# A reordered set-up and an earlier GRN total in a tuned ConvNeXt-V2 block on one Trainium2 core

## The chip, the cores and the metric

The kernel runs on one core of one Trainium2 chip. The metric is device time of one execution in microseconds (us). Each kernel is executed several times, and a median and a range are given. TensorE is called PE in the profile (PEld is its weight load), VectorE DVE, ScalarE ACT, GpSimd POOL, SyncE SP. The three queues that issue transfers here are SPq, ACTq and POOLq.

## The reference, cut to what matters

```python
# x: 1 x 512 x 512 x 96, bfloat16; dw 3x3x96; w1 96x384; w2 384x96
h = depthwise_conv3x3(x, dw)
h = layernorm(h)                     # over the 96 channels, no scale or shift
h = gelu_tanh(h @ w1)                # 96 -> 384
gx = sqrt(sum(h*h over H, W) + 1e-6) # one number per channel, over the whole image
nx = gx / (mean(gx) + 1e-6)
h = gamma * (h * nx) + beta + h      # GRN
return x + h @ w2
```

GRN is the knot: no output can be made before every pixel has passed the GELU.

## The kernel before

The image is cut into 128 blocks of four rows. **Phase 1** (to about 990 us) runs a software pipeline with one block a slot: x is transposed by DVE (`turn_x`), PE convolves with tap weights (`Wq`, three bursts of 24 matmuls), ACT copies the result to `y_bf` and squares it, PE sums both into `SG`, a short chain makes the reciprocal deviation `rstd`, and the norm multiplies `y_bf` by `rbc`, the deviation spread to all channels. The first four blocks (the ramp) spread `rstd` through PE; later ones send it out to DRAM (`r_dram`) and read it back broadcast (`rbc`). The normed block goes through DRAM into `ynT`, and the first expansion (`w1p`) and the GELU follow. **Phase 2** recomputes some expansions, multiplies by `W2s` (w2 with the GRN scale) into `O`, adds the residual `xb` made by POOL, and writes.

The parts that the change touches (cut):

```python
FILL = (6, 24)                       # dummy matmuls that keep PE's clock up
...
act.dma_start(out=dw9[:], ...)
for b in range(2): load_x(b)         # on the SP queue
# w1, w2, gamma, beta by act.dma_start, then the GELU table warm-up
for b in range(2, 4): load_x(b)
make_identity(nc, ident_f[:])
pool.memset(Wq[:], 0.0)
for t in yn_ring:                    # six tiles, zero rows 96..127
    pool.dma_start(out=t[C:128, :, :], in_=zrow[...])
...
n += 1                               # twelve tap copies Wd -> Wq
(dve if n % 2 else pool).tensor_copy(out=Wq[...], in_=Wd[...])
...
def setup_mlp():                     # called after slot 1
    dve.memset(w1p[C:128, :], 0.0)
    Us = psY.tile([128, NI, W], f32, name="Y")   # the convolution's own PSUM tile
    # w1m, b2_ps by PE; w1p and B2bc_f copied out by DVE
...
def stage_norm(b):                   # every block
    pool.tensor_tensor(out=yn[:], in0=ybf.pop(b)[:], in1=rbcs[k][...], op=ALU.mult)
...
for n in range(RES):                 # end of phase 1
    for f in recompute_units(ORDER[n]): f()
advance(LEAD, PRE)                   # lead expansions of phase 2
# then: sums over blocks, rsqrt, total over channels (PE), W2s, B2c, all on DVE
```

Of the kernel before, what the change touches and what calls it, by code (L numbers as in the profile page):

```python
# [8 lines left out]
ALU = mybir.AluOpType  # L9
# [3 lines left out]
GR = 4  # L13
# [3 lines left out]
FILL = (6, 24)  # L17
BATCH = 4
RES = 2
# [34 lines left out]
def kernel(  # L54
# [105 lines left out]
    with ExitStack() as p1:  # L160
# [8 lines left out]
        def banks(n):  # L169
            return (psU2 if n == 2 else psU1).tile([128, n, W], f32, name=f"U{n}")  # L170
# [33 lines left out]
        for b in range(min(2, NBLK)):  # L204
            load_x(b)
        for i in range(NI):
            act.dma_start(out=w1_raw[i:C:NI, :], in_=w1[chans(i), :])
# [4 lines left out]
        act.activation(out=warm[:], in_=warm[:], func=ACTF.Gelu_apprx_tanh)  # L212
        for b in range(2, min(4, NBLK)):
            load_x(b)
        make_identity(nc, ident_f[:])
        pool.memset(Wq[:], 0.0)
        for t in yn_ring:
            pool.dma_start(out=t[C:128, :, :], in_=zrow[C:128, None, :].to_broadcast([128 - C, GR, W]))
# [5 lines left out]
        dve.memset(cen[:], 1.0)  # L224
# [127 lines left out]

        busy(FILL[0])
# [9 lines left out]
        for h in range(2):  # L363
            for j in range(GR):
                for q in (2 * h, 2 * h + 1):
                    a = q + GR * shift(h, j) - j + 1
                    if 0 <= a < 3:
                        n += 1
                        (dve if n % 2 else pool).tensor_copy(out=Wq[32 * q:32 * q + 32, :, :, j, :],
                                        in_=Wd[32 * q:32 * q + 32, :, 3 * a:3 * a + 3, :])  # L370

        def setup_stats():
            dve.memset(SG[:], 0.0)
            dve.memset(rowsel[:], 0.0)
            for j in range(GR):
                dve.memset(rowsel[32 * j:32 * j + 32, j:j + 1], 1.0)

        def setup_mlp():
            dve.memset(w1p[C:128, :], 0.0)
            Us = psY.tile([128, NI, W], f32, name="Y")  # L380
            w1m, b2_ps = Us[:, 0, :E], Us[:, 1, :C]
            pe.matmul(w1m, lhsT=cen[:], rhs=w1_raw[:], start=True, stop=True)
            for j in range(NCH):
                pe.matmul(b2_ps, lhsT=bet_bf[:, j:j + 1].to_broadcast([128, 128]), rhs=w2_sb[:, j, :],
                          start=(j == 0), stop=(j == NCH - 1))
            dve.scalar_tensor_tensor(out=w1p[:C, :], in0=w1m[:C], scalar=-1.0 / C, in1=w1_raw[:],
                                     op0=ALU.mult, op1=ALU.add)
            dve.tensor_copy(out=B2bc_f[:], in_=b2_ps)
# [200 lines left out]
        def stage_norm(b):  # L589
            k = batch_of[b]  # L590
            b0, n = BATCHES[k]
            yn = ynpool.tile([128, NI, W], bf16, name="yn")
            pool.tensor_tensor(out=yn[:], in0=ybf.pop(b)[:],
                               in1=rbcs[k][:, b - b0:b - b0 + 1, :].to_broadcast([128, NI, W]), op=ALU.mult)
            yns[b] = yn
# [132 lines left out]
        setup_stats()  # L728
        store = None
        for s in range(last_slot + 1):  # L730
# [26 lines left out]
            def spread_out():  # L757
                for k in get("spread"):
                    stage_spread(k)
                for b in get("norma"):  # L760
                    stage_norm(b)
# [67 lines left out]
            if s == 1:  # L829
                setup_mlp()  # L830
# [17 lines left out]
        if store:  # L848
            store()
        for j in range(NCH):  # L850
            junk = bstpool.tile([128, 128], f32, name="junk")
            dve.scalar_tensor_tensor(out=junk[:], in0=gram[:, j, :], scalar=1.0, in1=ident_f[:],
                                     op0=ALU.mult, op1=ALU.mult, accum_out=diag[:, j:j + 1])

        for n in range(RES):
            for f in recompute_units(ORDER[n]):
                f()
        made[0] = RES * UPB
    with p2:
        late.psU2 = p2.enter_context(tc.tile_pool(name="psU2", bufs=2, space=bass.MemoryType.PSUM))  # L860
        dve2, pe2, psO = dve, pe, late.psO
        advance(LEAD, PRE)
        gsm = p2.enter_context(tc.tile_pool(name="gsm", bufs=1))
        m2 = gsm.tile([128, NCH, NACC], f32, name="m2")
        dve2.tensor_tensor(out=m2[:], in0=mv[:, :, :, 0], in1=mv[:, :, :, 0], op=ALU.mult)
        dve2.tensor_tensor(out=m2[:], in0=m2[:], in1=mv[:, :, :, 1], op=ALU.add)
        dve2.tensor_tensor(out=m2[:], in0=m2[:], in1=npx[:, None, :].to_broadcast([128, NCH, NACC]), op=ALU.mult)
        ssq = gsm.tile([128, NCH], f32, name="ssq")
        dve2.tensor_reduce(out=ssq[:], in_=m2[:], axis=AX.X, op=ALU.add)
        dve2.scalar_tensor_tensor(out=ssq[:], in0=ssq[:], scalar=GRN_EPS, in1=diag[:], op0=ALU.add, op1=ALU.add)  # L870
        gi = gsm.tile([128, NCH], i32, name="gi")
        dve2.tensor_scalar(out=gi[:], in0=ssq[:].bitcast(i32), scalar1=-0.5, scalar2=float(0x5F3759DF),
                                op0=ALU.mult, op1=ALU.add)
        r = gi[:].bitcast(f32)
        for it in range(3):
            t_ = gsm.tile([128, NCH], f32, name=f"gt{it}")
            dve2.scalar_tensor_tensor(out=t_[:], in0=r, scalar=-0.5, in1=r, op0=ALU.mult, op1=ALU.mult)
            dve2.tensor_tensor(out=t_[:], in0=t_[:], in1=ssq[:], op=ALU.mult)
            rn_ = gsm.tile([128, NCH], f32, name=f"gr{it}")
            dve2.scalar_tensor_tensor(out=rn_[:], in0=t_[:], scalar=1.5, in1=r, op0=ALU.add, op1=ALU.mult)  # L880
            r = rn_[:]
        gx = gsm.tile([128, NCH], f32, name="gx")
        rs_ = gsm.tile([128, 1], f32, name="rs_")
        dve2.scalar_tensor_tensor(out=gx[:], in0=ssq[:], scalar=1.0, in1=r, op0=ALU.mult, op1=ALU.mult,
                                       accum_out=rs_[:])
        tot_ps = psO.tile([128, GPS, C], f32, name="O")[:, 0, 0:1]
        pe2.matmul(tot_ps, lhsT=ones_f[:], rhs=rs_[:], start=True, stop=True)
        den = gsm.tile([128, 1], f32, name="den")
        dve2.tensor_scalar(out=den[:], in0=tot_ps, scalar1=1.0 / E, scalar2=GRN_EPS,
                                op0=ALU.mult, op1=ALU.add)  # L890
        gg = gsm.tile([128, NCH], f32, name="gg")
        dve2.tensor_tensor(out=gg[:], in0=gx[:], in1=gam[:], op=ALU.mult)
        rden = gsm.tile([128, 1], f32, name="rden")
        dve2.reciprocal(out=rden[:], in_=den[:])
        sc = gsm.tile([128, NCH], f32, name="sc")
        dve2.tensor_scalar(out=sc[:], in0=gg[:], scalar1=rden[:, 0:1], scalar2=1.0, op0=ALU.mult, op1=ALU.add)
        for j in range(NCH):
            dve2.tensor_scalar(out=W2s[:, j, :], in0=w2_sb[:, j, :], scalar1=sc[:, j:j + 1], scalar2=None,
                                    op0=ALU.mult)
        dve2.tensor_copy(out=B2c[:], in_=B2bc_f[:])  # L900

        def out_part(q, o_sb, sub):
            r0 = q * GR
            nc.sync.dma_start(
                out=out[0, r0:r0 + GR].rearrange("r w c -> (r w) c").rearrange(
                    "(p g) c -> p g c", g=PXP)[:, sub * GPS:(sub + 1) * GPS],
                in_=o_sb[:, sub * GPS:(sub + 1) * GPS])
# [44 lines left out]
```

## Time and profile before

| What | us |
|---|---|
| median of three runs (range) | 1537.59 (1536.48 to 1541.44) |
| span of the profiled run | 1529.2 |
| third spread of `rstd` (end of the ramp, "spread 2") | 42.00 |
| first product of phase 2 ("first O") | 995.94 |
| from first O to the end | 533.3 |

Such milestones are read from the timeline: the start of one named group of instructions, in us from the start of the span. They let a gain be followed through the run. The profiled run was faster than any of the three timed ones. The lines of this profile stand in the prediction.

### The profile page before, as it was taken

The numbers are of one execution on the slowest core, as the hardware profiler recorded it, in microseconds if no ns is written. First come the engines' busy times: TensorE is split into PE (matmuls) and PEld (weight loads), VectorE is DVE, ScalarE is ACT, GpSimd is POOL, SyncE is SP. The second block draws the span as 40 slices with busy tenths as digits, with TensorE's granted clock in tenths as the row PEclk, the third lists the DMA queues.
The fourth block names the chain that finished last, engine by engine and source line by source line (L and its number), as shares of the span: only waits on it lengthen the run. The fifth ranks groups of instructions, "written<-read, shape, count | busy, mean of one in ns | idle before, by whom it ended". The sixth has DMA issues, their size and how long they took to land.

```text
span 1529.2 us, 54880 instructions
## 1 busy us (share of the span) xinstructions
PE 1420.8 (93%) x23119; PEld 815.8 (53%) x23119; DVE 1201.7 (79%) x2157; ACT 1450.9 (95%) x1692; POOL 1315.5 (86%) x933
## 2 busy tenths in 40 slices
PE   7899999999999999999999987799999999999998
PEld 3344444444444444444444443377777666676676
DVE  6859989999999999999999999855555555455555
ACT  3989999999999999999999999999999999999997
POOL 3559899999999989989899987189999999899997
PEclk8999999999999999999999999999999999999999
DMA  5668787788888778787778667789999999999996
GB/s 149 188 185 260 233 257 242 241 260 248 246 255 249 242 236 257 231 269 241 225 238 261 216 204 237 262 279 392 383 382 387 377 380 376 355 377 377 380 379 234
DMA packets 235469, 427.89 MB, mean 280 GB/s; under 512 B 34102, under 2 KB 148374, under 8 KB 235222
## 3 DMA queue, kind: packets, MB, share of 16 engines
q1 hardware_dynamic: 219972, 356.59, 71.9%
q0 software_dynamic: 13888, 67.64, 11.7%
q8 instruction: 181, 2.97, 0.8%
q14 instruction: 66, 0.54, 0.1%
q10 hardware_dynamic: 1362, 0.15, 0.1%
HBM read 272.78 MB, written 150.72 MB: 277 GB/s over the span
## 4 chain that ended last, share of the span: by engine, by line
POOL 24%; PE 21%; ACT 21%; DMA 10%; DVE 8%; issue 5%; SPq 3%; POOLq 0%; ACTq 0%
POOL xb L287 14%; PE U L32 10%; ACT gsh L32 10%; PE O L32 8%; ACT gm L32 6%; DVE bst L32 5%; ACT y_bf L32 4%; DMA yn_dram<-yn 4%; SPq L32 3%; POOL yn L32 3%; POOL ysq L32 3%; DMA ynT<-yn_dram 2%; PE Y L32 2%; POOL xr L255 2%; DMA xin<-in_x_dram 2%
## 5 line engine op out<-in xcount | busy, mean ns | idle before, releaser
L32 PE MATMUL U<-ynT,w1p 128*128 128x512 bf16 x2292 | 652.4, 381 | 36.5 <-ACT gsh L32 8.9
L32 ACT ACTIVATE gr<-U 128x1536 bf16<-128x1536 f32 (+1 forms) x386 | 520.1, 1448 | 15.2 <-PE U L32 14.3
L32 DVE BATCH_NORM_STATS2 bst<-gsh 128x6 f32<-128x512 bf16 x756 | 464.9, 672 | 29.3 <-ACT gsh L32 27.9
L32 DVE TENSOR_TENSOR o_sb<-O,xb 128x384 bf16<-128x384 f32 x512 | 277.4, 556 | 252.0 <-PE O L32 148.0
L32 POOL TENSOR_TENSOR yn<-y_bf,rbc 128x1536 bf16<-128x1536 bf16 x128 | 397.4, 3107 | 84.3 <-DMA rbc<-r_dram 31.5
L32 ACT ACTIVATE gm<-U 128x512 bf16<-128x512 f32 (+1 forms) x640 | 417.5, 795 | 13.8 <-PE U L32 13.7
L287 POOL TENSOR_TENSOR xb<-xr,B2c 128x1536 f32<-128x1536 bf16 x126 | 394.7, 3134 | 37.9 <-DVE B2c L32 33.6
L32 ACT ACTIVATE gsh<-U 128x1024 bf16<-128x1024 f32 x504 | 375.7, 875 | 3.7 <-ACT gm L32 1.9
L32 PE MATMUL Y<-xT,Wq 64*32 64x511 bf16 (+1 forms) x8694 | 323.5, 390 | 25.1 <-ACT y_bf L32 5.7
L32 POOL TENSOR_TENSOR ysq<-y_bf 128x1536 bf16<-128x1536 bf16 x114 | 313.2, 2748 | 11.8 <-ACT y_bf L32 11.8
L32 PEld LDWEIGHTS <-w1p 128*128 128x128 bf16 x2292 | 182.7, 98 | 241.7 <-issue 153.5
L32 PEld LDWEIGHTS <-gr 128*128 128x128 bf16 x4584 | 236.2, 98 | 108.1 <-issue 22.9
L32 PE MATMUL O<-W2s,gr 128*128 128x96 bf16 x4584 | 256.6, 206 | 13.1 <-DVE o_sb L32 12.7
L32 DVE BATCH_NORM_STATS2 bst<-gm 128x6 f32<-128x512 bf16 x378 | 234.3, 674 | 0.8 <-ACT gm L32 0.8
L32 PEld LDWEIGHTS <-Wq 64*32 64x32 bf16 x9216 | 112.7, 90 | 203.4 <-issue 152.9
L32 ACT ACTIVATE y_bf<-Y 128x1536 bf16<-128x1536 f32 x121 | 186.6, 1542 | 17.1 <-PE Y L32 16.0
L32 DVE STREAM_TRANSPOSE xT<-xin 128x576 f32<-128x576 f32 (+1 forms) x256 | 181.2, 747 | 2.5 <-DMA xin<-in_x_dram 2.5
L32 PEld LDWEIGHTS <-gm 128*128 128x128 bf16 x1560 | 99.2, 98 | 103.4 <-issue 71.5
L32 PE MATMUL SG<-gm 128*128 128x128 bf16 x1560 | 130.3, 220 | 19.1 <-DVE SG L32 18.8
L32 PE MATMUL U<-w1p,ynT 128*128 128x384 bf16 (+2 forms) x780 | 127.7, 273 | 1.4 <-ACT resg L32 0.2
L255 POOL DMA_DIRECT2D xr<-in_x_dram x123 | 68.1, 553 | 35.9 <-POOL xb L287 35.9
L32 PE MATMUL O<-W2s,gl 128*128 128x96 bf16 x1512 | 84.9, 206 | 0.0
(103 smaller groups left out, 678.4 us busy)
## 6 DMA issues: line engine op xcount, KB each, us to landing
ynT<-yn_dram SPq DMA_DIRECT2D x254, 384.0 KB
xin<-in_x_dram SPq DMA_DIRECT2D x126, 432.0 KB
yn_dram<-yn SPq DMA_DIRECT2D x512, 96.0 KB
xr<-in_x_dram POOLq DMA_DIRECT2D x128, 384.0 KB, 6.5
out_dram<-o_sb SPq DMA_DIRECT2D x127, 384.0 KB
g_dram<-gsh SPq DMA_DIRECT2D x126, 384.0 KB
gl<-g_dram SPq DMA_DIRECT2D x84, 384.0 KB
gl<-g_dram POOLq DMA_DIRECT2D x42, 384.0 KB, 7.2
```

The costliest lines, as they stand in the source:

```text
L32: r = f(*a, **k)
L255: pq.dma_start(out=xr[:], in_=x[0, r0:r0 + GR].rearrange("r w c -> (r w) c").rearrange("(p g) c -> p g c", g=PXP))
L287: pq.tensor_tensor(out=xb[:], in0=grp[q]["xr"][:], in1=bias[:, None, :].to_broadcast([128, PXP, C]), op=ALU.add)
```

## The change

The set-up is reordered so that nothing delays the first convolutions: x loads are issued first; the zero rows move behind POOL's tap copies; ACT clears `Wq` and takes six of the twelve tap copies; fewer dummy matmuls run; the mlp set-up moves two slots later and into a PSUM bank of its own; the norms of blocks 0 and 1 go to DVE. At the joint of the phases, the GRN total goes ahead of the last resident expansion. The diff, cut to its core:

```diff
-FILL = (6, 24)
+FILL = (6, 17)
...
+        act.activation(out=warm[:], ...Gelu)            # table load first
+        act.activation(out=Wq[...], in_=zrow[...], func=ACTF.Identity)
+        for b in range(2, min(4, NBLK)):
+            load_x(b)
         # w1, w2, gamma, beta loads on ACT's queue
-        for b in range(2, min(4, NBLK)):
-            load_x(b)
-        pool.memset(Wq[:], 0.0)
-        for t in yn_ring:
-            pool.dma_start(out=t[C:128, :, :], in_=zrow[C:128, None, :]...)
...
-                        (dve if n % 2 else pool).tensor_copy(...)
+                        if n % 2:   act.activation(out=o, in_=i_, func=ACTF.Identity)
+                        elif n % 4: dve.tensor_copy(out=o, in_=i_)
+                        else:       pool.tensor_copy(out=o, in_=i_)
+        def setup_ynt():      # the zero rows, called after slot 0
...
         def setup_mlp():
-            Us = psY.tile([128, NI, W], f32, name="Y")
+            Us = banks(1)[:, 0, :]
...
-                    stage_norm(b)
+                    stage_norm(b, dve if b < 2 else pool)
...
-            if s == 1:
+            if s == 0:
+                setup_ynt()
+            if s == 3:
                 setup_mlp()
...
+        # sums, rsqrt and gx on DVE, before any recomputed expansion
+        ahead = [f for n in range(RES) for f in recompute_units(ORDER[n])]
+        for f in ahead[:-1]:
+            f()
+        # total (PE), den, W2s, B2c
+        ahead[-1]()
         ...
         advance(LEAD, PRE)
```

More of the change, by code (lines that the diff above doesn't have):

```diff
@@ L205 @@
             load_x(b)
+        act.activation(out=warm[:], in_=warm[:], func=ACTF.Gelu_apprx_tanh)
+        act.activation(out=Wq[:].rearrange("p i d j c -> p (i d j c)").rearrange("p (a w) -> p a w", a=3),
+                       in_=zrow[:, None, :NI * GR * 32].to_broadcast([128, 3, NI * GR * 32]), func=ACTF.Identity)
+        for b in range(2, min(4, NBLK)):
+            load_x(b)
         for i in range(NI):
@@ L211 @@
             act.dma_start(out=bet_bf[:], in_=grn_beta.rearrange("(j p) -> p j", p=128))
-        act.activation(out=warm[:], in_=warm[:], func=ACTF.Gelu_apprx_tanh)
-        for b in range(2, min(4, NBLK)):
-            load_x(b)
         make_identity(nc, ident_f[:])
-        pool.memset(Wq[:], 0.0)
-        for t in yn_ring:
-            pool.dma_start(out=t[C:128, :, :], in_=zrow[C:128, None, :].to_broadcast([128 - C, GR, W]))
         dve.tensor_copy(out=ident_b[:], in_=ident_f[:])
@@ L223 @@
         cen = consts.tile([C, 128], bf16, name="cen")
-        dve.memset(cen[:], 1.0)
         xtpool = pc.enter_context(tc.tile_pool(name="xt", side="right", bufs=1))
@@ L351, in busy @@
                 pe.matmul(J[:, k % NI, :], lhsT=zrow[:, :128], rhs=zrow[:], start=True, stop=True)
+        pool.memset(rowsel[:], 0.0)
+        for j in range(GR):
+            pool.memset(rowsel[32 * j:32 * j + 32, j:j + 1], 1.0)
+        pool.memset(cen[:], 1.0)
+        pool.memset(w1p[C:128, :], 0.0)
+        dve.memset(SG[:], 0.0)
         busy(FILL[0])
@@ L368 @@
                         n += 1
-                        (dve if n % 2 else pool).tensor_copy(out=Wq[32 * q:32 * q + 32, :, :, j, :],
-                                        in_=Wd[32 * q:32 * q + 32, :, 3 * a:3 * a + 3, :])
-        def setup_stats():
-            dve.memset(SG[:], 0.0)
-            dve.memset(rowsel[:], 0.0)
-            for j in range(GR):
-                dve.memset(rowsel[32 * j:32 * j + 32, j:j + 1], 1.0)
+                        o, i_ = Wq[32 * q:32 * q + 32, :, :, j, :], Wd[32 * q:32 * q + 32, :, 3 * a:3 * a + 3, :]
+                        if n % 2:
+                            act.activation(out=o, in_=i_, func=ACTF.Identity)
+                        elif n % 4:
+                            dve.tensor_copy(out=o, in_=i_)
+                        else:
+                            pool.tensor_copy(out=o, in_=i_)
+        def setup_ynt():
+            for t in yn_ring:
+                pool.dma_start(out=t[C:128, :, :], in_=zrow[C:128, None, :].to_broadcast([128 - C, GR, W]))
         def setup_mlp():
-            dve.memset(w1p[C:128, :], 0.0)
-            Us = psY.tile([128, NI, W], f32, name="Y")
-            w1m, b2_ps = Us[:, 0, :E], Us[:, 1, :C]
+            Us = banks(1)[:, 0, :]
+            w1m, b2_ps = Us[:, :E], Us[:, E:E + C]
             pe.matmul(w1m, lhsT=cen[:], rhs=w1_raw[:], start=True, stop=True)
@@ L587, in stage_bcast, with stage_norm @@
             rbcs[k] = rbc
-        def stage_norm(b):
+        def stage_norm(b, eng=None):
             k = batch_of[b]
@@ L592, in stage_norm @@
             yn = ynpool.tile([128, NI, W], bf16, name="yn")
-            pool.tensor_tensor(out=yn[:], in0=ybf.pop(b)[:],
+            (eng or pool).tensor_tensor(out=yn[:], in0=ybf.pop(b)[:],
                                in1=rbcs[k][:, b - b0:b - b0 + 1, :].to_broadcast([128, NI, W]), op=ALU.mult)
@@ L727 @@
         turn_x(1)
-        setup_stats()
         store = None
@@ L849 @@
             store()
+        gsm = p2.enter_context(tc.tile_pool(name="gsm", side="right", bufs=1))
+        m2 = gsm.tile([128, NCH, NACC], f32, name="m2")
+        dve.tensor_tensor(out=m2[:], in0=mv[:, :, :, 0], in1=mv[:, :, :, 0], op=ALU.mult)
+        dve.tensor_tensor(out=m2[:], in0=m2[:], in1=mv[:, :, :, 1], op=ALU.add)
+        dve.tensor_tensor(out=m2[:], in0=m2[:], in1=npx[:, None, :].to_broadcast([128, NCH, NACC]), op=ALU.mult)
+        ssq = gsm.tile([128, NCH], f32, name="ssq")
+        dve.tensor_reduce(out=ssq[:], in_=m2[:], axis=AX.X, op=ALU.add)
         for j in range(NCH):
@@ L853 @@
                                      op0=ALU.mult, op1=ALU.mult, accum_out=diag[:, j:j + 1])
-        for n in range(RES):
-            for f in recompute_units(ORDER[n]):
-                f()
-        made[0] = RES * UPB
-    with p2:
-        late.psU2 = p2.enter_context(tc.tile_pool(name="psU2", bufs=2, space=bass.MemoryType.PSUM))
-        dve2, pe2, psO = dve, pe, late.psO
-        advance(LEAD, PRE)
-        gsm = p2.enter_context(tc.tile_pool(name="gsm", bufs=1))
-        m2 = gsm.tile([128, NCH, NACC], f32, name="m2")
-        dve2.tensor_tensor(out=m2[:], in0=mv[:, :, :, 0], in1=mv[:, :, :, 0], op=ALU.mult)
-        dve2.tensor_tensor(out=m2[:], in0=m2[:], in1=mv[:, :, :, 1], op=ALU.add)
-        dve2.tensor_tensor(out=m2[:], in0=m2[:], in1=npx[:, None, :].to_broadcast([128, NCH, NACC]), op=ALU.mult)
-        ssq = gsm.tile([128, NCH], f32, name="ssq")
-        dve2.tensor_reduce(out=ssq[:], in_=m2[:], axis=AX.X, op=ALU.add)
-        dve2.scalar_tensor_tensor(out=ssq[:], in0=ssq[:], scalar=GRN_EPS, in1=diag[:], op0=ALU.add, op1=ALU.add)
+        dve.scalar_tensor_tensor(out=ssq[:], in0=ssq[:], scalar=GRN_EPS, in1=diag[:], op0=ALU.add, op1=ALU.add)
         gi = gsm.tile([128, NCH], i32, name="gi")
-        dve2.tensor_scalar(out=gi[:], in0=ssq[:].bitcast(i32), scalar1=-0.5, scalar2=float(0x5F3759DF),
+        dve.tensor_scalar(out=gi[:], in0=ssq[:].bitcast(i32), scalar1=-0.5, scalar2=float(0x5F3759DF),
                                 op0=ALU.mult, op1=ALU.add)
@@ L876 @@
             t_ = gsm.tile([128, NCH], f32, name=f"gt{it}")
-            dve2.scalar_tensor_tensor(out=t_[:], in0=r, scalar=-0.5, in1=r, op0=ALU.mult, op1=ALU.mult)
-            dve2.tensor_tensor(out=t_[:], in0=t_[:], in1=ssq[:], op=ALU.mult)
+            dve.scalar_tensor_tensor(out=t_[:], in0=r, scalar=-0.5, in1=r, op0=ALU.mult, op1=ALU.mult)
+            dve.tensor_tensor(out=t_[:], in0=t_[:], in1=ssq[:], op=ALU.mult)
             rn_ = gsm.tile([128, NCH], f32, name=f"gr{it}")
-            dve2.scalar_tensor_tensor(out=rn_[:], in0=t_[:], scalar=1.5, in1=r, op0=ALU.add, op1=ALU.mult)
+            dve.scalar_tensor_tensor(out=rn_[:], in0=t_[:], scalar=1.5, in1=r, op0=ALU.add, op1=ALU.mult)
             r = rn_[:]
@@ L883 @@
         rs_ = gsm.tile([128, 1], f32, name="rs_")
-        dve2.scalar_tensor_tensor(out=gx[:], in0=ssq[:], scalar=1.0, in1=r, op0=ALU.mult, op1=ALU.mult,
+        dve.scalar_tensor_tensor(out=gx[:], in0=ssq[:], scalar=1.0, in1=r, op0=ALU.mult, op1=ALU.mult,
                                        accum_out=rs_[:])
-        tot_ps = psO.tile([128, GPS, C], f32, name="O")[:, 0, 0:1]
-        pe2.matmul(tot_ps, lhsT=ones_f[:], rhs=rs_[:], start=True, stop=True)
+        ahead = [f for n in range(RES) for f in recompute_units(ORDER[n])]
+        for f in ahead[:-1]:
+            f()
+        tot_ps = late.psO.tile([128, GPS, C], f32, name="O")[:, 0, 0:1]
+        pe.matmul(tot_ps, lhsT=ones_f[:], rhs=rs_[:], start=True, stop=True)
         den = gsm.tile([128, 1], f32, name="den")
-        dve2.tensor_scalar(out=den[:], in0=tot_ps, scalar1=1.0 / E, scalar2=GRN_EPS,
+        dve.tensor_scalar(out=den[:], in0=tot_ps, scalar1=1.0 / E, scalar2=GRN_EPS,
                                 op0=ALU.mult, op1=ALU.add)
         gg = gsm.tile([128, NCH], f32, name="gg")
-        dve2.tensor_tensor(out=gg[:], in0=gx[:], in1=gam[:], op=ALU.mult)
+        dve.tensor_tensor(out=gg[:], in0=gx[:], in1=gam[:], op=ALU.mult)
         rden = gsm.tile([128, 1], f32, name="rden")
-        dve2.reciprocal(out=rden[:], in_=den[:])
+        dve.reciprocal(out=rden[:], in_=den[:])
         sc = gsm.tile([128, NCH], f32, name="sc")
-        dve2.tensor_scalar(out=sc[:], in0=gg[:], scalar1=rden[:, 0:1], scalar2=1.0, op0=ALU.mult, op1=ALU.add)
+        dve.tensor_scalar(out=sc[:], in0=gg[:], scalar1=rden[:, 0:1], scalar2=1.0, op0=ALU.mult, op1=ALU.add)
         for j in range(NCH):
-            dve2.tensor_scalar(out=W2s[:, j, :], in0=w2_sb[:, j, :], scalar1=sc[:, j:j + 1], scalar2=None,
+            dve.tensor_scalar(out=W2s[:, j, :], in0=w2_sb[:, j, :], scalar1=sc[:, j:j + 1], scalar2=None,
                                     op0=ALU.mult)
-        dve2.tensor_copy(out=B2c[:], in_=B2bc_f[:])
+        dve.tensor_copy(out=B2c[:], in_=B2bc_f[:])
+        ahead[-1]()
+        made[0] = RES * UPB
+    with p2:
+        late.psU2 = p2.enter_context(tc.tile_pool(name="psU2", bufs=2, space=bass.MemoryType.PSUM))
+        advance(LEAD, PRE)
         def out_part(q, o_sb, sub):
```

## The prediction

> **What bounds the kernel now.** I read the page first (busy shares, the 40 slices), then the timeline of the first 45 us, the DMA view of single microseconds there, busy time by stage, and the chain of waits around the change of phase.
>
> The page of the kernel before, part 1:
> ```profile
> PE 1420.8 (93%) x23119; PEld 815.8 (53%) x23119; DVE 1201.7 (79%) x2157; ACT 1450.9 (95%) x1692; POOL 1315.5 (86%) x933
> ```
> There are two phases. From about 100 to 975 us (convolution, norm, first expansion) the busy table by stage gives DVE 98% and ACT 98% between 200 and 400 us: rate bound. After 996 us (second product and output) PE, ACT and POOL are each above 91% in every stretch that I took from 1036 to 1510. The change alters no instruction of either steady stretch. It can gain only in the start, where nothing is full, and at the joint of the phases.
>
> The timeline of the start of the kernel before (start us, us, engine, line, operation, count, idle time before and its releaser):
> ```profile
> 2.36 3.44 POOL L32 DMA_DIRECT2D ynT<-zrow  x6
> 7.08 1.44 DVE L32 STREAM_TRANSPOSE xT<-xin 128x576 f32<-128x576 f32 x2
> 10.99 1.44 DVE L32 STREAM_TRANSPOSE xT<-xin 128x576 f32<-128x576 f32 x2 [2.48 <-DMA xin<-in_x_dram]
> 11.82 0.40 PE L32 MATMUL Y<-xT,Wq 64*32 64x512 bf16 x3 [1.18 <-DVE xT L32]
> ...
> 14.39 2.86 PE L32 MATMUL U<-xT,Wq 64*32 64x512 bf16 x72
> ...
> 22.15 4.42 PE L32 MATMUL Y<-xT,Wq 64*32 64x512 bf16 x72 [3.68 <-DVE B2bc_f L32]
> 26.50 0.40 PE L32 MATMUL U<-ident_b,rstdx 128*128 128x128 bf16 x4
> 27.68 3.12 POOL L32 TENSOR_TENSOR yn<-y_bf,rbc 128x1536 bf16<-128x1536 bf16 x1 [19.26 <-ACT rbc L32]
> 27.88 2.95 DVE L32 SCALAR_TENSOR_TENSOR var<-mom 128x16 f32<-128x16 f32 x1
> ...
> 40.28 0.82 PE L32 MATMUL U<-ynT,w1p 128*128 128x512 bf16 x3
> 42.00 0.61 PE L32 MATMUL U<-ident_b,rstdx 128*128 128x128 bf16 x8
> ```
> The first convolution, ready to run at 10.10, is held to 11.82 by x block 1. The third is held to 22.15 because the mlp set-up occupies its PSUM tile until B2bc_f is copied out. The spread of block 0's rstd stands behind it at 26.50. At 27.88 a 16-column DVE operation takes 2.95 us, against 0.16 us for the same operation ten us earlier, exactly under the POOL norm. The first expansion is at 40.28 and the third spread at 42.00.
>
> The DMA view of 5 to 6 us, by queue (packets, MB, share of 16 engines):
> ```profile
> q0 software_dynamic: 64, 0.15, 54.9%
> q10 hardware_dynamic: 635, 0.07, 51.2%
> ```
> q0 is POOL's zero rows (6 x 128 KB), q10 the weights, gamma and beta. The x queue does not appear: SP's wait list shows one 2.8 us wait for the w1 load, and SP issues block 1 only at 5.30. Zero rows held 87% in the microsecond before, 79% in the one after.
>
> The timeline of the joint:
> ```profile
> 989.12 0.16 DVE L32 SCALAR_TENSOR_TENSOR gx<-ssq,gr 128x3 f32<-128x3 f32 x1
> 992.01 2.72 PE L32 MATMUL U<-ynT,w1p 128*128 128x512 bf16 x6 [1.11 <-ACT gr L32]
> 994.52 0.43 PE L32 MATMUL O<-rs__23273,ones_f 128*128 128x1 f32 x2
> 995.64 0.56 DVE L32 TENSOR_SCALAR W2s<-w_sb,sc 128x96 bf16<-128x96 bf16 x3
> 995.94 1.27 PE L32 MATMUL O<-W2s,resg 128*128 128x96 bf16 x12 [0.99 <-DVE W2s L32]
> ```
> The row sums exist at 989.3, but the total is queued on PE behind the lead expansions. The chain of waits then runs on PE until 1035 and on POOL afterwards:
> ```profile
> 1035.52 0.57 DVE o_sb L32
> 1036.09 3.13 POOL xb L287
> ```
>
> **The Trainium skill.** "DMA: Bandwidth & Descriptors", Queues, rings and completion order: an engine round-robins between the queues that have work, packet by packet, so zero rows and x share bandwidth. The q0 lines agree. "VectorE: DVE Perf Modes", The perf-mode tier table: a bf16 tensor_tensor in SBUF runs at 2x (1224 ns for 2048 columns, with some 150 cycles fixed). My estimate for 1536 columns is (768 + 150)/0.96 = 0.96 us; no such operation is in this trace, where POOL takes 3.12. "ScalarE: Activation LUTs", What ACT_TABLE_LOAD costs: 186 ns + 0.833 ns a column, 93 ns overlapped; the trace's 128x1024 activation at 1.02 us agrees. "TensorE: Matmul & The Clock Gate", Part 1: an idle window of about 3.4 us halves the PE clock. The trace agrees: after the 3.7 us idle 72 convolution matmuls took 4.42 us, and 2.85 where the clock was whole; the mean grant from 20 to 40 us was 0.76.
>
> **The change part by part.**
> (1) x first. x1 no longer waits for w1 and should be issued at about 2. The x queue had moved 0.44 MB (block 0) by 4 us, and reaches 0.41 MB in its best microsecond (12 to 13), so x1 should land near 5.5 instead of 10.99. The zero rows (0.79 MB) go behind POOL's tap copies, to about 6.6 to 10 us.
> (2) Taps. Zeroing Wq moves to ACT: 186 + 0.833 x 1152 = 1.15 us beside its DMA issues. Of twelve 32x288 copies, DVE keeps three (0.27 each, 0.8 less on DVE), POOL three, ACT takes six: 0.43 each alone, about 2.1 together. ACT issues its six weight and beta loads before them, one of which waits for x1, so I expect the copies to end near 8.4. DVE transposes x0 to about 7.6 and x1 to 9.0; its SG clear (0.48) is earlier and the rowsel clears leave it. The filler, 17 x 0.256 from 4.02, ends at 8.4 too. Convolution 0 then runs 8.5 to 11.4, against an end at 14.68: 3.3 us earlier. That is the sum of 1.7 from x1 and 1.6 from the shorter filler.
> (3) mlp set-up in another bank, two slots later. The third convolution follows the statistics: convolution 1 ends at 14.2, statistics at 14.9, convolution 2 at 17.8. The stage's DVE chain (2.87 us from mom to rstdx in the trace) ends at 17.9, so spread 0 comes at about 17.9, not 26.50: 8.6 earlier. Of that 3.3 is from (2), 3.7 the wait, 1.5 the clock.
> (4) Norms 0 and 1 on DVE: 0.96 each instead of 3.12, and POOL no longer stalls the 2.95 us operation. But block 4's transpose now queues behind norm 0: rbc 18.35 to 18.95, norm to 19.9, transposes to 21.4. So convolution 3 waits to about 20.7 and ends at 23.3 (before 30.4; 7.1 earlier). Chain 1 on DVE: 21.4 to 24.3, x5 to 25.7; convolution 4 to 27.9. ACT's rbc 1 at 26.9, norm 1 27.9, w1p and B2bc_f 28.6 (set-up now on DVE's path), x6 30.1. First expansion about 30.4. Chain 2, 3.4 us, ends at 33.5: spread 2 at 33.5 against 42.00, 8.5 us earlier. From here everything is relative to the slots, so I carry 8.5.
> (5) Joint. The total goes ahead of the last resident expansion, which waits for ACT until 989.89 anyway; W2s is ready by about 992. The lead expansions still end at 994.73, and O follows at once instead of at 995.94: 1.2 us. xb for block 2 starts earlier too, but the next xb waits for an output buffer, so POOL gains no more.
> Sum: 8.5 + 1.2 = 9.7; 1537.6 - 9.7 = 1527.9.
>
> **Rivals.** (a) ACT becomes the bound of the set-up: if its DMA issues (3.6 us) wait for the table load, clear and x1, the copies end at 9.7, costing 1.2: about 1529. For it: issues took the ACT queue from 0.73 to 5.07. Against: they need not wait for ACT's datapath. (b) DVE becomes the ramp's bound, with norms and w1p serial before transposes; if a norm runs at 1x (1.7 us) and PE goes cold while waiting (1.5 us a convolution), 3 to 4 us return: 1531. (c) The start's gain is absorbed by slack in slots 6 to 20: the busy table shows DVE only 33% and ACT 74% in 80 to 100, with POOL waiting for a load there. Were that stretch set by DMA round trips, 5 us or more could vanish: 1533 to 1536. I doubt it, since these are also started by the slots before. (d) More: later phases of waits fall better, 1523.
>
> **Range and chances.** These put 8 in 10 between 1522 and 1533. Faster by 2% needs 1506.8, 31 us, three times all I find. Slower by 2% would need a new steady cost, and no steady instruction changed.
>
> **What would show it.** x1's first transpose near 8 with no DMA wait; convolution 0 ending at 11 to 12; no PE wait for B2bc_f; DVE norms below 1.2 us; spread 2 at 33 to 35; the phase joint (first O) some 10 us earlier, at 985 to 987; den, W2s no longer between lead expansions and O; 533 us from there to the end as before. It is wrong if the offset at spread 2 has shrunk or grown by several us at the joint, or if the second phase changes its length.

## The result, and the profile after

| | median us | range | runs |
|---|---|---|---|
| before | 1537.28 | 1536.48 to 1541.44 | 4 |
| after | 1531.92 | 1531.30 to 1532.50 | 4 |

The ratio is 0.996 (95% interval 0.9941 to 0.9978). A ratio is the mean time of one kernel's runs over that of the other's of the same rounds, so it isn't quite the ratio of the medians. The change is 5.4 us faster, within 2%: inside the predicted range, but 5.4 is little more than half of the 9.7 predicted. (A second measurement of the same two kernels, below, gave 7.7.) All outputs are right.

The page of the changed kernel, busy time by engine (part 1) and two DMA queues (part 3: packets, MB, share of 16 engines):

```profile
PE 1421.2 (93%) x23112; PEld 816.3 (53%) x23112; DVE 1199.4 (78%) x2149; ACT 1453.7 (95%) x1699; POOL 1309.4 (86%) x934
...
q8 instruction: 181, 2.97, 0.8%
q14 instruction: 67, 0.54, 0.1%
```

Part 1 is the same within 0.5% on every engine, so no steady work changed. The two `instruction` queues are not data: they come up again below.

The timeline of the start of the changed kernel (start us, us, engine, line, operation, count, idle time before and its releaser):

```profile
6.38 5.39 DVE L32 STREAM_TRANSPOSE xT<-xin 128x576 f32<-128x576 f32 x8
6.78 0.38 ACTq L32 DMA_DIRECT2D bet_bf<-in_grn_beta_dram  x1
6.82 3.46 POOL L32 DMA_DIRECT2D ynT<-zrow  x6
7.27 2.47 ACT L32 ACTIVATE Wq<-Wd 32x288 bf16<-32x288 bf16 x6 [3.31 <-DVE xT L32]
...
16.14 1.40 PE L32 MATMUL Y<-xT,Wq 64*32 64x512 bf16 x26
...
19.81 1.85 PE L32 MATMUL Y<-xT,Wq 64*32 64x512 bf16 x46 [2.27 <-issue]
...
21.59 0.40 PE L32 MATMUL U<-ident_b,rstdx 128*128 128x128 bf16 x4
...
22.66 0.96 DVE L32 TENSOR_TENSOR yn<-y_bf,rbc 128x1536 bf16<-128x1536 bf16 x1 [3.53 <-ACT rbc L32]
...
24.36 4.02 PE L32 MATMUL U<-xT,Wq 64*32 64x512 bf16 x66 [1.27 <-DVE xT L32]
...
35.53 0.82 PE L32 MATMUL U<-ynT,w1p 128*128 128x512 bf16 x3
...
37.92 0.73 PE L32 MATMUL U<-ident_b,rstdx 128*128 128x128 bf16 x8 [0.76 <-DVE rstdx L32]
```

Four things of the plan are there: the transposes run in one piece from 6.38 (no wait for x block 1), no convolution waits for `B2bc_f`, the DVE norm takes 0.96 us, and the 2.95 us DVE operation is gone. Three things are new. ACT's tap copies start only at 7.27, behind the issue of the beta load. The third convolution breaks off after 26 of its 72 matmuls, and PE stands for 2.27 us with nothing to wait for that the profile shows ("issue"). And the next convolution runs 66 matmuls in 4.02 us, half speed for a part of it: PE's mean clock from 20 to 30 us was 0.83. Spread 2 is at 37.92, not at 33.5.

The timeline of the joint of the phases, changed kernel:

```profile
992.16 0.56 PE L32 MATMUL O<-rs__23216,ones_f 128*128 128x1 f32 x2 [0.55 <-issue]
993.41 0.56 DVE L32 TENSOR_SCALAR W2s<-w_sb,sc 128x96 bf16<-128x96 bf16 x3
994.17 3.10 POOL L285 TENSOR_TENSOR xb<-xr,B2c 128x1536 f32<-128x1536 bf16 x1 [29.84 <-DVE B2c L32]
994.70 2.72 PE L32 MATMUL U<-ynT,w1p 128*128 128x512 bf16 x6 [1.11 <-ACT gr L32]
997.21 0.99 PE L32 MATMUL O<-W2s,resg 128*128 128x96 bf16 x12
```

The total and `W2s` are done by 993.97, before the lead expansions even begin, and `O` follows them without a gap. In the kernel before, `O` waited 0.99 us for `W2s` at this place. The total has a small price that the prediction did not count: PE waits 0.55 us for it, ahead of the last resident expansion. The chain of waits, changed kernel, where it leaves PE for POOL:

```profile
1156.67 0.66 PE U L32 x3
...
1157.88 3.14 POOL xb L285
```

In the kernel before this hand-over was at 1036. Its place says little, though: from first O to the end the changed kernel takes 532.3 us against 533.3.

**A trap.** The first O of the two profiled runs is at 995.94 before and at 997.21 after. By these two traces the change is a loss at this point, and the two spans are 1529.2 and 1529.5. The medians say 5.4 us. So one of the two profiled runs was no typical one.

### The profile page after: what moved, and what is told of

It reads as the page before. It is cut to its first block, busy times and chain, and to the rows that moved or that the text cites. A ratio compares the mean times of both kernels' runs of the same rounds, so it can differ in the third digit from the quotient of the medians. Undisturbed runs are those within 1.5% of the kernel's fastest.

```text
span 1529.5 us, 54869 instructions
## 1 busy us (share of the span) xinstructions
PE 1421.2 (93%) x23112; PEld 816.3 (53%) x23112; DVE 1199.4 (78%) x2149; ACT 1453.7 (95%) x1699; POOL 1309.4 (86%) x934
## 3 DMA queue, kind: packets, MB, share of 16 engines
q8 instruction: 181, 2.97, 0.8%
## 4 chain that ended last, share of the span: by engine, by line
PE 27%; POOL 16%; ACT 15%; DMA 7%; DVE 7%; issue 4%; SPq 3%; POOLq 0%; ACTq 0%
PE U L32 13%; PE O L32 11%; POOL xb L285 10%; ACT gsh L32 7%; DVE bst L32 4%; ACT gm L32 4%; ACT y_bf L32 3%; DMA yn_dram<-yn 3%; SPq L32 3%; PE Y L32 3%; DMA ynT<-yn_dram 2%; POOL yn L32 2%; POOL xr L253 1%; POOL ysq L32 1%; DMA rbc<-r_dram 1%
## 5 line engine op out<-in xcount | busy, mean ns | idle before, releaser
L32 ACT ACTIVATE gr<-U 128x1536 bf16<-128x1536 f32 (+1 forms) x386 | 519.2, 1449 | 14.1 <-PE U L32 13.1
L32 POOL TENSOR_TENSOR yn<-y_bf,rbc 128x1536 bf16<-128x1536 bf16 x126 | 391.2, 3108 | 89.9 <-ACT rbc L32 29.6
```

The source lines that it names most:

```text
L32: r = f(*a, **k)
```

## The experiments

**Theories.** T1: the gain at the end is the gain of the start plus that of the joint, and the start gained less than predicted because of new waits in it (the break in the third convolution, late tap copies). T2 (the prediction's rival c): the start gained as much as it should, and slack later took it back. T3: the parts disturb each other.

### The two kernels again, and each half of the change alone

`e1_before_again` and `e2_after_again` have no edit. `e3_joint_only` is the kernel before with only the last part of the change (GRN sums, total, `W2s` ahead of the last resident expansion); `e4_start_only` is the changed kernel with only that part undone:

```diff
 # e4_start_only, against the changed kernel (cut)
-        # sums, rsqrt, total, W2s, B2c ahead of ahead[-1]()
+        for n in range(RES):
+            for f in recompute_units(ORDER[n]): f()
+        advance(LEAD, PRE)
+        # sums, rsqrt, total, W2s, B2c here, as before
```

> The kernel before, unchanged, as a null and a second trace. Its own earlier runs spread from 1531.0 (the profiled one) to 1541.4 us. Both theories: ratio 1.000. If the first phase has a variable stretch, this trace's joint (first O matmul) lies several us from the 995.9 of the first trace, while the start (spread 2 at 42.0) repeats within 0.5 us. Theory A (the start's gain is 4 us and lasts) says that the first trace of before was a lucky one and most put the joint near 1001. Theory B (the gain is absorbed between slots 6 and 20) says the joint repeats at 996.

> The changed kernel, unchanged, second trace. Both theories: ratio 0.996. Spread 2 repeats at 37.9 within 0.5. Theory A: the joint stays at about 997. Theory B: a POOL wait for the rbc rows of about 9 us near 100 us and a stall of PE on ysq of about 4 us near 118 us are there again, whatever the start gained.

> The kernel before with only the GRN total moved ahead of the last expansion. My step (5): 1.2 us less, ratio 0.9992; in the trace W2s is ready before the lead expansions and the first O follows them at once. Rival: the second phase is POOL paced and gives some of it back, 0 to 0.5 us; or the earlier xb of block 2 adds to it, 2 us.

> The changed kernel with the joint as it was before. Theory A: 4 us less than before, ratio 0.9973, spread 2 at 37.9. Theory B: under 1.5 us less, ratio above 0.999, with spread 2 at 37.9 all the same.

The four ran beside the same 11 runs of the kernel before, whose median was 1537.52:

| | median us (range) | ratio (95%) | spread 2 | first O | first O to end |
|---|---|---|---|---|---|
| e1_before_again | 1535.11 (1533.90 to 1542.29) | 0.9993 (0.9970 to 1.0015) | 43.2 | 1008.5 | 532.0 |
| e2_after_again | 1529.80 (1527.98 to 1531.49) | 0.9947 (0.9929 to 0.9966) | 37.6 | 994.3 | 532.5 |
| e3_joint_only | 1536.21 (1531.83 to 1537.32) | 0.9983 (0.9962 to 1.0003) | 42.8 | 1003.2 | 532.2 |
| e4_start_only | 1533.51 (1530.55 to 1537.14) | 0.9973 (0.9953 to 0.9992) | 39.6 | 999.2 | 533.6 |

The same program as before came to its first O at 1008.5 instead of 995.94: its timing varies by 12 us from run to run, all of it in phase 1. So the first profile of before was a lucky run, and a single pair of traces can't measure a change of 5 us here. Some expectations were missed: spread 2 moved by 1.2 us in e1 (0.5 was expected at most) and stood at 39.6 in e4 (37.9 was expected), and e1's first O was expected near 1001. What can be compared is spread 2, which varies less. The three traces with the old start have it at 42.0, 43.2 and 42.8 (mean 42.7); those of the changed start at 37.9, 37.6, 39.6 and, in the last experiment below, 40.1 (mean 38.8). The start gained 3.9 us, not 8.5. The joint's 1.2 is too small to be certain in the medians (the interval of e3 includes 1), but it can be read inside the traces: from the last but one group of resident expansions to first O, PE took 7.75, 7.96 and 7.76 us with the old joint (before, e1, e4) and 6.51 and 6.84 with the new one (e3 and the changed kernel; 6.14 to 6.85 in e5 to e12). In e2 it took 4.99, with a whole PE clock at this place and not a half one as in the changed kernel, so e2 is left out of this comparison. 3.9 + 1.2 = 5.1 is near the 5.4 of the first measurement; this second one gave 7.7 (1537.52 to 1529.80), so the sum is no proof. The halves' ratios (0.9983 and 0.9973) also add up to between the two measured for the whole. T3 isn't needed, and T1 is ahead of T2.

### One part of the start at a time

`e5_zeros_late`: the zero rows wait for the first `rstd`, so they move after the first x loads have landed.

```diff
         def setup_ynt():
+            pool.tensor_copy(out=zgate[:], in_=rns[0][0:1, 0, 0, 0, 0:1])
             for t in yn_ring:
...
-            if s == 0:
+            if s == 1:
                 setup_ynt()
```

> The changed kernel with its six zero-row DMAs held back on POOL until the first rstd is there (about 19 us), when the x loads are done. Theory F: the 2.0 to 2.3 us in which PE stands still in convolution 2 (after 26 of its 72 matmuls, put down to issue) is the fetch of its own instructions: the instruction queue's first 16 KB block after the start moves at 17.4 us, in the stream of x loads and zero rows. Then the stall falls below 0.7, convolution 3 runs at the whole clock (2.9 us instead of 4.0 for its last 66), and spread 2 comes at 34.5 to 36 instead of 37.9. Rival: the stall has to do with PE's own queue or with a wait that the trace hides; then it stays at 2 us, and spread 2 at 37.5 to 38.

`e6_gb_after_taps`: the gamma and beta loads are issued by ACT after its tap copies.

```diff
-            act.dma_start(out=gam_bf[:], ...); act.dma_start(out=bet_bf[:], ...)   # ahead of the taps
...
+            act.dma_start(out=gam_bf[:], ...); act.dma_start(out=bet_bf[:], ...)   # behind them
```

> The changed kernel with the gamma and beta loads issued by ACT after its six tap copies and not before. Theory: ACT's queue stood until x1 had landed before the beta load could be issued (6.78), so the copies ran 7.27 to 9.74 and not 5.4 to 7.9. Then the copies start at 5.4 to 5.8, convolution 0's y_bf copy starts at 11.3 to 11.8 instead of 12.74, and spread 0 at 20.2 to 21.6. Rival: the DVE transposes of x1 are as late (7.8 to 9.3), then y_bf moves by under 0.5.

`e7_turn_first`: in slot 2 DVE transposes block 4 ahead of norm 0, the queueing that the prediction's part (4) had put a price on.

```diff
+                if s == 2:
+                    turn_x(s + 2)
                 if not spare:
                     spread_out()
...
-                if s + 2 < NBLK:
+                if s + 2 < NBLK and s != 2:
                     turn_x(s + 2)
```

> The changed kernel with DVE's transposes of block 4 ahead of norm 0, not behind it. Theory (my step 4): the norm put in front costs convolution 3 the 1.27 us wait for xT; without it the wait is gone, convolution 3 ends 1.3 to 2.5 earlier (28.38 before) and spread 2 is at 36.3 to 37.2. Rival: nothing, since the statistics chain on DVE behind it sets the next spread: spread 2 at 37.9.

`e8_norm_on_pool`: norms 0 and 1 back on POOL.

```diff
-                    stage_norm(b, dve if b < 2 else pool)
+                    stage_norm(b, pool)
```

> The changed kernel with norms 0 and 1 back on POOL. Theory (step 4): the norm takes 3.1 us again but x4's transposes are no longer behind it; the DVE operation under it is stretched to about 3 us, and spread 2 comes 0.5 to 2.5 later, 38.4 to 40.4. Rival: DVE is the scarce engine in the ramp, and POOL idle, so it is equal or faster: 36 to 38.

These four ran beside 7 runs of the kernel before with a median of 1538.66:

| | median us (range) | ratio (95%) | PE's break in conv 2 | spread 2 |
|---|---|---|---|---|
| e5_zeros_late | 1527.31 (1525.72 to 1529.15) | 0.9931 (0.9912 to 0.9950) | none | 34.4 |
| e6_gb_after_taps | 1530.90 (1529.15 to 1532.21) | 0.9953 (0.9934 to 0.9972) | 2.54 | 37.2 |
| e7_turn_first | 1530.10 (1528.11 to 1533.71) | 0.9951 (0.9929 to 0.9973) | 3.37 | 38.2 |
| e8_norm_on_pool | 1530.82 (1528.80 to 1533.34) | 0.9949 (0.9926 to 0.9972) | 2.28 | 38.5 |

Only moving the zero rows does much at spread 2; the intervals of the ratios overlap. The timeline of e5_zeros_late at the same place:

```profile
16.21 3.05 PE L32 MATMUL Y<-xT,Wq 64*32 64x512 bf16 x72
...
19.38 3.46 POOL L32 DMA_DIRECT2D ynT<-zrow  x6
...
22.01 2.82 PE L32 MATMUL U<-xT,Wq 64*32 64x512 bf16 x66 [1.27 <-DVE xT L32]
...
34.44 0.73 PE L32 MATMUL U<-ident_b,rstdx 128*128 128x128 bf16 x8 [0.82 <-DVE rstdx L32]
```

The third convolution runs its 72 matmuls in one piece, and the next one 66 in 2.82 us instead of 4.02. Two costs went at once: the break itself, and the half clock behind it (mean clock from 20 to 30 us: 1.00 against 0.83).

What was PE waiting for in "issue"? Queue q8, called "instruction" in the page, moved 181 packets and 2.97 MB in the run. The Trainium skill ("Trainium Architecture — The Big Picture", The software stack) says that instructions are 64 bytes. PE has 23,112 matmuls and as many weight loads: 46,224 x 64 bytes = 2.96 MB. So q8 agrees in size with PE's instruction stream. q14, 0.54 MB, agrees with all the others: 54,869 instructions in all less 46,224 are 8,645, x 64 bytes = 0.55 MB. PE's program therefore seems to come in during the run in blocks of 16.4 KB (2.97 MB by 181), through the same DMA engines as the data. Here are the queues from 17 to 18 us in the changed kernel, the microsecond in which q8's first packet moves:

```profile
q1 hardware_dynamic: 109, 0.33, 93.1%
q8 instruction: 1, 0.02, 6.9%
q0 software_dynamic: 1, 0.00, 0.1%
```

and from 14 to 15 us in e5_zeros_late, where it moves there:

```profile
q1 hardware_dynamic: 99, 0.31, 78.0%
q8 instruction: 1, 0.02, 5.8%
```

q1 carries x, q0 the zero rows, which in the changed kernel used the engines from 8 us on beside x (33% of them from 14 to 17 us, with q1 at 70%). Over the traces of all experiments the two go together. Where the first q8 packet moved between 16 and 18 us (the changed kernel, e2, e4, e6, e7, e8 and the later e12), PE broke off for 1.7 to 3.4 us; where it moved between 13 and 15 us (e5 and the later e9, e10 and e11, all with late zero rows), it stood for 0.2 us at most. Windows of 0.1 us show more. In all seven traces with a break, PE stopped after the same 26th matmul, and started again 2.4 to 2.6 us after that packet began to move (17.4 and 19.81 in the changed kernel, 18.0 and 20.57 in e7). Even the short stop of 0.16 us in e10 comes after the 26th matmul and ends 2.3 us after its packet (14.1 and 16.44). So the late block is very likely what stopped PE, though the profile doesn't record which matmuls came with which packet. In e5 x alone, with 78% of the engines beside the packet, did not hold it past 14.3 us. Whether the zero rows do so by themselves or only together with x was not tried.

e6 shows the other new wait. ACT's copies started at 5.42 instead of 7.27, and the first `y_bf` at 11.81 instead of 12.74; but PE still restarted at about the same time (19.2) after its break, so nothing was left of it at the third convolution (spread 0 came at 21.88, not at 20.2 to 21.6 as expected), and of the 0.7 us at spread 2 little can be told from scatter. e7 showed no gain, with a break of 3.37 us in its trace. e8 brought back what the norms on DVE had removed. Its timeline:

```profile
23.75 3.11 POOL L32 TENSOR_TENSOR yn<-y_bf,rbc 128x1536 bf16<-128x1536 bf16 x1 [13.49 <-ACT rbc L32]
...
23.99 2.90 DVE L32 SCALAR_TENSOR_TENSOR var<-mom 128x16 f32<-128x16 f32 x1
```

Both end within 0.03 us of each other (26.86 and 26.89): the 16-column DVE operation is let go when POOL's ends. The Trainium skill ("SBUF — State Buffer", Who interferes with whom) calls the port pair that the two engines share an exclusive lock, and this trace agrees. Its price for the ramp was 0.6 to 0.9 us at spread 2 (38.5 against 37.9 and 37.6), within the scatter of the changed start.

### The parts together, and the stall behind the ramp

`e9_zeros_and_gb` is e5 and e6 together. `e10_and_turn` adds e7. `e11_and_norm8_dve` adds to e10 the norms of blocks 4 to 7 on DVE:

```diff
             for b in get("norm"):
-                stage_norm(b)
+                stage_norm(b, dve if b < 8 else pool)
```

> The changed kernel with both repairs, zero rows after the first rstd and gamma and beta after the tap copies. If these two are all that separates my step-4 figure (spread 2 at 33.5) from what the changed kernel shows (37.6 to 37.9), the two effects add: no stall in convolution 2, y_bf 0 at 11.8, spread 2 at 33.2 to 33.9. If the fetch stall comes back in another place or the tap copies no longer matter, 34.4 as with the zero rows alone. Total: 0.991 to 0.994 of before, the slots from 4 to 8 giving back 3 to 6 us as in every trace but the first.

> The same with block 4's transposes ahead of norm 0. Alone it did nothing (38.2), as PE stood in the fetch stall. Theory: with the stall gone the 1.27 us wait of convolution 3 for xT shows, so spread 2 comes 0.8 to 1.5 earlier than in the run before. Rival: the DVE statistics chain behind it sets spread 2, no gain.

> The same with norms 4 to 7 on DVE too (it is a third busy there). Theory G: the loss of 3 to 6 us between blocks 4 and 8 is POOL's: its norms of batch 3 hold SP's queue of writes and the rows of rstd, so that the broadcast rows of batch 4 land only at 107, and POOL is then 4 us late with ysq. Then the rows of rstd go out 3 to 6 us earlier, PE's 4 us wait for ysq near 118 shrinks below 1.5, and the whole is 3 to 5 us faster than the run before. Rival: the loss is the DMA round trip's own, or DVE pays it back in its near-full first phase: within 1.5 us of the run before.

They ran beside 11 runs of the kernel before with a median of 1535.64:

| | median us (range) | ratio (95%) | spread 2 | first O |
|---|---|---|---|---|
| e9_zeros_and_gb | 1526.58 (1521.22 to 1527.59) | 0.9935 (0.9915 to 0.9955) | 33.6 | 990.6 |
| e10_and_turn | 1525.55 (1523.12 to 1527.54) | 0.9931 (0.9914 to 0.9947) | 32.7 | 992.5 |
| e11_and_norm8_dve | 1522.77 (1518.05 to 1527.92) | 0.9914 (0.9892 to 0.9936) | 32.3 | 983.5 |

With both new waits removed, spread 2 is at 33.6, the 33.5 of the prediction, and the median is 9.1 us below that of before, against 9.7 predicted. e7's edit, worth nothing by itself, moved spread 2 by 0.9 once the break was gone; the medians of e9 and e10 don't tell the two apart.

e11 follows another trail. Nearly every trace shows a stall behind the ramp, at about 115 to 130 us. It is seen best in the spacing of the gram products of successive blocks on PE (`SG<-gm`, which sum the squares of the GELU's outputs for GRN), which is 7.0 us in the steady stretch. From block 5 to block 6 it was 13.4 in the changed kernel, 12.7 in e2, 12.6 in e1, and 11.5 to 13.8 in e3 to e10. In the first profile of before it was 7.4. So the stall is in the traces of both kernels, and its absence gave that run 5.2 of the 12.5 us by which it was ahead of e1 at first O. The timeline of the changed kernel shows PE in it:

```profile
122.21 0.48 PE L32 MATMUL SG<-rowsel,ysq 128*128 128x4 bf16 x12 [4.33 <-POOL ysq L32]
```

PE waits for a square that POOL makes, and POOL is late because its next norm waits for `rbc`. Those rows go out late on SP's queue, behind the writes of the norms that POOL has been making at 3.1 us each. The timeline of e10_and_turn:

```profile
92.12 1.16 SPq L32 DMA_DIRECT2D r_dram<-rt  x2
...
98.28 3.33 SPq L32 DMA_DIRECT2D rbc<-r_dram  x4
...
104.05 3.11 POOL L32 TENSOR_TENSOR yn<-y_bf,rbc 128x1536 bf16<-128x1536 bf16 x1 [8.38 <-DMA rbc<-r_dram]
```

and of e11_and_norm8_dve, whose norms 4 to 7 took 0.92 to 0.96 us on DVE:

```profile
87.30 1.17 SPq L32 DMA_DIRECT2D r_dram<-rt  x2
...
93.33 1.98 SPq L32 DMA_DIRECT2D rbc<-r_dram  x4
...
97.77 3.11 POOL L32 TENSOR_TENSOR yn<-y_bf,rbc 128x1536 bf16<-128x1536 bf16 x1 [15.37 <-DMA rbc<-r_dram]
```

The rows go out 4.8 us earlier (0.4 of it from the earlier start), and block 8's norm runs 6.3 us earlier. The spacing from block 5 to block 6 is 7.0 us: no stall. Its median is the lowest of all, 2.8 us below e10's (3 to 5 were expected); its interval still overlaps that of e10.

`e12_after_norm8_dve` tests this alone, on the changed kernel itself, with the same one-line edit and nothing else:

> The changed kernel with one edit: the norms of blocks 4 to 7 on VectorE, as the norms of blocks 8 and later stay on GpSimd. Theory that the changed kernel's start is given back between blocks 4 and 8 because GpSimd's norms (3.1 us each) hold back the r_dram rows of the next group: the loss of 5 to 6 us that both traces of the changed kernel show between blocks 4 and 8 goes (offset of block 8 against the first before trace no later than that of block 4, about -5 us), TensorE's wait on ysq of 3.3 to 4.3 us there becomes 0.5 us or less, the joint's first product comes at 987 to 991 us instead of 994 to 997, and the median is 1525 to 1528 us. Rival, that the edit helped only because the start of that other kernel was already 5 us earlier (or that what it showed was a lucky run): the loss between blocks 4 and 8 stays at 3 us or more, and the median stays at 1529 to 1532 us. Spread 2 should not move in either (37 to 38 us).

It took 1526.46 us (1525.53 to 1528.93, 5 runs) beside 1536.34 for the kernel before (9 runs): ratio 0.9935 (0.9922 to 0.9949). The spacing from block 5 to block 6 is 7.0 us, and the wait for the square is not there; both were as the theory said, and so was the median. Two numbers missed: first O came at 994.55, not at 987 to 991, and spread 2, which should have stayed at 37 to 38, was at 40.1. This profiled run was the slowest of its five (1528.93), and its start was slow: PE stood 1.74 us in the third convolution, and its mean clock from 20 to 30 us was 0.53, although the edit begins behind that. So in the changed kernel the stall is a cost of POOL's norms behind the ramp; on the kernel before the edit was not tried. What it is worth in time is less certain. Against the kernel before of the same rounds, e12 gains 9.9 us and the changed kernel gained 5.4 and 7.7, which leaves 2 to 4.5 us for the edit, but the intervals overlap; between e10 and e11 it is 2.8 us. In the traces the spacing shrinks by 4.5 to 6.8 us. Why it is sometimes missing, as in the first profile of before, stays open.

## Why the prediction was right or wrong

**The result** was in the range, and "within 2%" was right. The central figure, 1527.9, was 4.0 us too low.

**The joint, part (5), held.** The prediction was that `O` follows the lead expansions at once, 1.2 us earlier; it does. Inside the traces the new joint saves 0.9 to 1.8 us (6.14 to 6.85 us against 7.75 to 7.96, e2 left out). Alone it measured 0.9983, which is 2.6 us with an interval that includes 0 and 1.2.

**The DVE norm and the waits that were to go, parts (1), (3) and (4), held.** The norm took the estimated 0.96 us, x block 1 was no longer waited for, `B2bc_f` held no convolution, and the stretched DVE operation went away with the POOL norm and came back with it (e8).

**The step that failed is the sum of the start, "spread 2 at 33.5 against 42.00, 8.5 us earlier".** It measured 3.9 us (means of four and three traces). Its working followed two things only, the data of each engine and the order of its instructions, and two terms were missing:

1. *"The third convolution follows the statistics: ... convolution 2 ends at 17.8."* It began at 16.14 and ended at 21.66, since PE stopped for 2.27 us and then ran the next convolution partly at half clock. The prediction counted 1.5 us of gain from a whole clock; the slow stretch took 1.2 of that back (66 matmuls in 4.02 us against 2.82 in e5). The prediction, by the TensorE page of the skill that it cites, has a half clock follow an idle window of about 3.4 us; here breaks of 1.74 to 3.37 us were enough in all seven traces that have one, with the half clock between 18 and 35 us, while e5, e9, e10 and e11 had a whole clock there. Moving the zero rows away from this moment (e5) removed the break and the slow clock, and gave 3.5 us at spread 2 (37.9 to 34.4). In the three traces of the old start the first q8 packet moved at 14.8 to 16.0 us, behind the zero rows (over by 11.2), and PE stood idle for `B2bc_f` until 22.15 or later anyway, so a break would have been hidden. Nothing in that profile showed the risk but the two "instruction" lines of the page.
2. *"So I expect the copies to end near 8.4."* They ended at 9.74. This was rival (a), "the copies end at 9.7, costing 1.2", named with the right figure but held unlikely: ACT's queue can't go on to the copies before it has issued the beta load, and that issue came at 6.78. The copies themselves took 2.47 us, against about 2.1. e6 moved the copies to 5.42, and with the break gone too (e9) spread 2 came to 33.6.

With both terms removed the predicted mechanism gives about what was predicted: 33.6 at spread 2 and 9.1 us in the median. That 33.6 and 33.5 agree so closely is in part luck: in e9 spread 0 came at 18.48 (predicted 17.9) and the first expansion at 31.19 (30.4), 0.6 to 0.8 us late, and a shorter last step made it up.

**Rival (b)**, DVE as the bound of the ramp with a cold PE, is half right. PE was cold, but the break was the reason and not DVE: the norm ran at the estimated rate, and e5, with the same 1.27 us wait for DVE's transpose but no break, had a whole clock. That its figure, 1531, is close to the measured 1531.92 is luck. **Rival (c)**, absorption in slots 6 to 20, named the right stretch and the right cause (POOL waiting for a round trip through DRAM), but not the right effect: both kernels lose time there alike. The first gram product of block 6, behind the stall, begins at 128.1, 127.4 and 130.0 us in the traces of the changed start (changed kernel, e2, e4), and at 134.7 and 134.2 in e1 and e3. From there to first O 13 of the 14 traces take 866.9 to 869.9 us (e1: 873.8), so what is won by block 6 is kept. The gain of the start passes through. Only against the lucky first profile, with 127.3, does it look absorbed.

**The prediction's check list**: "the phase joint some 10 us earlier, at 985 to 987" was not to be had with a trace that varies by 12 us at that point; "533 us from there to the end as before" held within 1 us in every trace (532.0 to 533.6).

## What to carry to other kernels

When several loads and clears are moved into the first microseconds, the instruction stream of the busiest engine is very likely one more transfer that wants the same DMA engines: look for a stop of PE in "issue" and for the first packet of the "instruction" queue, and keep bulk transfers that aren't needed yet out of that moment. Before two traces are compared, run the old kernel a second time, and follow a milestone that scatters little. When an early gain seems to vanish later, look at whether the old kernel pays at the same place too: here that question led to the cheapest further gain, one engine swapped in the norms of four blocks.

The fastest version that ran, by its median, is e11_and_norm8_dve: 1522.77 us, 12.9 below the kernel before in the same rounds.

## What the Trainium skill lacked or had wrong

- "Trainium Architecture — The Big Picture", The software stack, says that the instruction streams are moved to the engines when the program is loaded. The trace shows packets of "instruction" queues during the whole execution: 181 on q8 (2.97 MB, the size of PE's 46,224 instructions) and 67 on q14 (0.54 MB), the first of q8 only at 13.5 to 18.0 us.
- "DMA: Bandwidth & Descriptors", Queues, rings and completion order, lists refill under row 14 and doesn't mention q8, the queue that agrees in size with PE's instructions here (2.97 MB; q14 has 0.54 MB).
- "Runtime: NRT & Kernel Launch", Instruction fetch mechanics, does describe a refill in blocks during the run and calls its cost mostly hidden; it has no figure for a block that comes late. In these runs PE stood for 1.7 to 3.4 us in the third convolution where the zero rows and x were moving at that time, and not at all in e5, where the zero rows came later.
- No page that I read tells how far one program's timing varies from run to run: the kernel before reached the same instruction at 995.9 and at 1008.5 us in two profiled runs, and its timed runs lie between 1532.7 and 1542.6.
